# The last two layers of a fused attention, expert and feed-forward kernel, regrouped: four token tiles a group, the middle values in chunks of 256, the sums of a group held in four banks of PSUM

## The chip, the cores and the metric

The kernel runs on one core of one Trainium2 chip. The metric is the device time of one execution in microseconds (us); lower is better. PE is TensorE's matmul queue, PEld its weight loads, DVE is VectorE, ACT ScalarE, POOL GpSimd and SP SyncE. Matmul results go to PSUM, which has eight banks of 512 float32 values in each of 128 partitions.

## The reference, cut to what matters

Three layers follow each other: a linear attention, a mixture of experts that picks two of eight experts for each token, and a dense feed-forward layer. The change is in the last.

```python
x = attention(q, k, v)                    # 2304 tokens of 512 values
x = mixture_of_experts(x)                 # top 2 of 8 experts, 512 -> 1024 -> 512
# the dense layer: w_in is 512 x 2048, w_out is 2048 x 512
h = x @ w_in
g = np.maximum(h, 0.0) + alpha * np.minimum(h, 0.0)
return (g @ w_out).astype(np.float32)
```

## The kernel before

The tokens are cut into 18 tiles of 128 rows, called T0 to T17. Every matrix product is made of three matmuls, since each operand is kept as a high part and a low part (`xh` and `xl`, `gh` and `gl`, `hi` and `lo`): high by high, low by high, high by low. The parts are written by two engines in turn: ACT rounds a value to its high part, then DVE or POOL subtracts that from the value to get the low part.

The dense layer has two steps. `ffn_in` multiplies the inputs by `w_in` and gives the 2048 middle columns in sixteen slices of 128, here called f0 to f15. Each slice is a block of twelve matmuls into one PSUM bank, with the weights held in the array and the tokens streaming past. Two DVE instructions read the bank (lines 940 and 941: the negative part, then the sum with the positive part, into a tile `neg`). ACT makes `gh` from `neg` (line 942) and POOL makes `gl` (line 943). `ffn_out` multiplies the middle values of one tile by `w_out`: 48 matmuls with a moving width of 512 into one bank, then ACT copies the sums to `y` and sends them to memory.

In the kernel before, a group is two tiles, so a matmul of `ffn_in` streams 256 columns, and nine groups follow each other. A group does all of `ffn_in` (192 matmuls), then `ffn_out` for its two tiles. All banks of sums come from a rotation of five (`acc_tile`), so that PE can be up to five slices ahead of DVE.

Between them lies the preparation of the next group. `gather_y` fetches for each tile the two expert outputs of its tokens, which are called a and b here, by indirect DMAs from POOL (tile name `xg`, four buffers). `mix` scales a on ACT (line 856) and adds b on DVE (line 857). `turn` transposes the sum on PE into `pt` and writes `xh` and `xl`.

Two more things happen beside the first group alone. The weights `w_out` are still to be split into high and low parts: eight pieces of 128 x 1024, a cast on ACT (line 165) and a subtraction on DVE or POOL (line 166) each. And `maybe_overflow` has every engine read a counter and branch, for the case that an expert got more tokens than its buffer holds; with these inputs the branch is not taken. An engine that passes the branch adjusts the semaphores for the work it skipped, so that a later wait for that engine can end only when it has passed too. In the code before, the branch is written in the middle of the second `ffn_out` of the first group.

After the expert layers the order on each engine is set by a scheduler that works on priorities in program order; it may move an instruction past others on its engine.

Of the kernel before, what the change touches and what calls it, by code (L numbers as in the profile page):

```python
# [8 lines left out]
F32 = mybir.dt.float32  # L9
# [13 lines left out]
LT = LOW // 128  # L23
# [3 lines left out]
EPS = 1e-9  # L27
NVA = 2
NKV = 6
TG = 2  # L30
GROUP = TG * 128
LAST = NT - 2
TINY = 1.125 * 2.0 ** -15

# [13 lines left out]
def r(ap):  # L48
    return ap.bitcast(F32R)
# [3 lines left out]
def attention_moe_ffn(ctx, tc, q, k, v, w_gate, w_noise, noise, w1, w2, w_in, w_out, alpha, out):  # L53
# [16 lines left out]
    turns, held = [0], [None]  # L70

    def acc_tile():

        if turns[0] % 5 == held[0]:
            turns[0] += 1
# [656 lines left out]
    def drain(share):  # L732

        credit[0] += share * credit[1]
        while fill and fill[0][0] <= credit[0] + 0.3:
            w, fn = fill.pop(0)
            credit[0] -= w
            fn()

    def split(i, vector=4):  # L740

        return [(1.14, lambda j=j: split_piece(i, j, nc.vector if j < vector else nc.gpsimd)) for j in range(4)]
# [96 lines left out]

        return [(0.94, one), (1.28, two), (0.6, three)]  # L840

    def gather_y(g):
        for c in range(TG):
            T = g * TG + c
            src = ys[0:E * LOW, :] if (T + 1) * 128 <= LOW else ys[0:E * CAP, :]
            for i in range(2):
                t = xg[g, c, i] = moe.tile([128, DM], F32, name="xg", bufs=4)
# [4 lines left out]
    def mix(g, c):  # L852

        T = g * TG + c
        a, b = xg[g, c, 0], xg.pop((g, c, 1))
# [3 lines left out]
    def turn(g, c):  # L859
        sl = slice(g % 2 * GROUP + c * 128, g % 2 * GROUP + (c + 1) * 128)  # L860
        split_t(xg.pop((g, c, 0)), xh[:, :, sl], xl[:, :, sl])

    doubles = [(i, j) for i in range(4) for j in range(8)] if wide else []
    pieces = list(doubles)
# [28 lines left out]
    for e in range(E):  # L893
        last = e + 1 == E
        plan(split(2 * e + 2), convert_next(3 if e else 0))
        if not last:
            fetch(e + 1, range(0 if e else LT, 4))
        if 0 < e < E - 1:
            expert_in(e, (0, 1))
        elif last:  # L900
            expert_in(e, [0])
            for c in range(LT):
                expert_out(e, c)
            gather_y(0)
            expert_in(e, [1])
        else:
            expert_in(e, [1])
        drain(9)
        plan(split(2 * e + 3), convert_next(3 if e else 0))
        for c in range(CT):  # L910
            prefetch(e + 1, c)
            if last and c == LT:
                for i in range(TG):
                    mix(0, i)
            elif last and c > LT:
                turn(0, c - LT - 1)
# [7 lines left out]
    early_cx.close()  # L924
    ffn = ctx.enter_context(tc.tile_pool(name="ffn", bufs=1))

    GT = []

    def ffn_in(g):
        GT[:] = [ffn.tile([128, F2 // 128, GROUP], F32, name=n) for n in ("gh", "gl")]  # L930
        xs0 = slice(g % 2 * GROUP, (g % 2 + 1) * GROUP)
        for f in range(F2 // 128):
            hi, lo = wt[2 * E + f // 8]
            acc = acc_tile()
            a = acc[:, :GROUP]
            mm3(a, [((hi[:, d * 1024 + f % 8 * 128:d * 1024 + f % 8 * 128 + 128],
                      lo[:, d * 1024 + f % 8 * 128:d * 1024 + f % 8 * 128 + 128]),
                     (xh[:, d, xs0], xl[:, d, xs0])) for d in range(4)])
            t = ffn.tile([128, GROUP], F32, name="neg", bufs=5)
            nc.vector.tensor_scalar(t, a, 0.0, alph[:, f:f + 1], op0=OP.min, op1=OP.mult)  # L940
            nc.vector.scalar_tensor_tensor(t, a, 0.0, t, op0=OP.max, op1=OP.add)  # L941
            nc.scalar.copy(r(GT[0][:, f, :]), t)  # L942
            nc.gpsimd.tensor_sub(r(GT[1][:, f, :]), t, GT[0][:, f, :])  # L943
            drain(0.08)

    def out_rows(T):
        hb, i = divmod(T, 9)
# [7 lines left out]
    def ffn_out(g, c, between={}):  # L955
        acc = acc_tile()
        cs = slice(c * 128, (c + 1) * 128)
        pairs = []
        for f in range(F2 // 128):
            hi, lo = wt[2 * E + 2 + f // 8]  # L960
            ws = slice(f % 8 * 512, (f % 8 + 1) * 512)
            pairs.append(((GT[0][:, f, cs], GT[1][:, f, cs]), (hi[:, ws], lo[:, ws])))
        mm3(acc, pairs, between)
        y = moe.tile([128, DM], F32, name="y", bufs=2)
        nc.scalar.copy(y, acc)  # L965
        for p, dst in out_rows(g * TG + c):
            nc.scalar.dma_start(dst, y[p])

    def overflow():


        wa = ffn.tile([128, 4096], F32, name="wa", tag="gh")
        wb = ffn.tile([128, 4096], F32, name="wb", tag="gl")
# [68 lines left out]
        for e in range(E):  # L1042
            n = nc.values_load(more[0:1, e:e + 1], min_val=0, max_val=MORE)
            with tc.For_i(0, n, 1) as tt:
                idx = ffn.tile([128, 2], I32, name="oidx")
                nc.sync.dma_start(idx, ls[bass.ds(e * ALL + CAP + tt * 128, 128), :])
                nc.sync.dma_start(wa.rearrange("p (a n) -> p a n", a=4),
                                  w1[e].rearrange("(a p) n -> p a n", p=128))
                nc.sync.dma_start(wb.rearrange("p (a n) -> p a n", a=8),
                                  w2[e].rearrange("(a p) n -> p a n", p=128))  # L1050
                x = moe.tile([128, DM], F32, name="y", bufs=2)
                nc.gpsimd.indirect_dma_start(out=x, out_offset=None, in_=xs[:, :],
                                             in_offset=bass.IndirectOffsetOnAxis(ap=idx[:, 0:1], axis=0))
                pt = ps.tile([128, 4, 128], F32, name="pt", bufs=2)
                for d in range(4):
                    nc.tensor.transpose(pt[:, d, :], x[:, d * 128:(d + 1) * 128], ident)
                xt = stage.tile([128, 4, 128], F32, name="oxt", tag="raw")
                nc.vector.tensor_copy(xt, pt)
                h = stage.tile([128, 8, 128], F32, name="oht", tag="raw")
                for f in range(8):  # L1060
                    acc = acc_tile()
                    for d in range(4):
                        nc.tensor.matmul(acc[:, 0:128], wa[:, d * 1024 + f * 128:d * 1024 + f * 128 + 128],
                                         xt[:, d, :], start=(d == 0), stop=(d == 3))
                    nc.scalar.activation(h[:, f, :], acc[:, 0:128], AF.Relu)
                acc = acc_tile()
                for f in range(8):
                    nc.tensor.matmul(acc, h[:, f, :], wb[:, f * 512:(f + 1) * 512],
                                     start=(f == 0), stop=(f == 7))
                y = moe.tile([128, DM], F32, name="y", bufs=2)  # L1070
                nc.scalar.copy(y, acc)
                nc.gpsimd.indirect_dma_start(
                    out=ys[:, :], out_offset=bass.IndirectOffsetOnAxis(ap=idx[:, 1:2], axis=0),
                    in_=y, in_offset=None)

    def maybe_overflow():
        n = nc.values_load(more[0:1, E:E + 1], min_val=0, max_val=MORE)
        at = turns[0]
        held[0] = (at - 1) % 5
        with tc.If(n > 0):  # L1080
            overflow()
        turns[0], held[0] = at, None

    for g in range(NTOK // GROUP):
        if g + 1 < NTOK // GROUP:
            gather_y(g + 1)
        if g == 0:
            plan(split(2 * E + 2) + split(2 * E + 3, 1))
        ffn_in(g)
        drain(9)  # L1090
        for c in sorted(range(TG), key=lambda c: g * TG + c == LAST):
            if g + 1 < NTOK // GROUP:
                mix(g + 1, c)
                turn(g + 1, c)
            ffn_out(g, c, {8: maybe_overflow} if g == 0 and c == TG - 1 else {})


_INS = ["q", "k", "v", "moe_w_gate", "moe_w_noise", "moe_noise", "moe_w1", "moe_w2",
# [22 lines left out]
```

## Time and profile before

| what | us |
|---|---|
| median of three runs | 995.37 |
| lowest and highest run | 994.95, 998.21 |
| the profiled execution, its time | 998.39 |
| its span, first to last instruction | 996.6 |
| its mean granted TensorE clock | 0.981 |

The profile shows the profiled execution, which is 3.02 us above the median; 1.79 us of its time lie outside its span. The dense layer begins 584.27 us after the first instruction.

### The profile page before, as it was taken

The numbers are of one execution on the slowest core, as the hardware profiler recorded it, in microseconds if no ns is written. First come the engines' busy times: TensorE is split into PE (matmuls) and PEld (weight loads), VectorE is DVE, ScalarE is ACT, GpSimd is POOL, SyncE is SP. The second block draws the span as 40 slices with busy tenths as digits, with TensorE's granted clock in tenths as the row PEclk, the third lists the DMA queues.
The fourth block names the chain that finished last, engine by engine and source line by source line (L and its number), as shares of the span: only waits on it lengthen the run. The fifth ranks groups of instructions, "written<-read, shape, count | busy, mean of one in ns | idle before, by whom it ended". The sixth has DMA issues, their size and how long they took to land. (4 is left out here: it accounts for less than half of the span.)

```text
span 996.6 us, 14925 instructions
## 1 busy us (share of the span) xinstructions
PE 953.0 (96%) x5882; PEld 860.0 (86%) x5882; DVE 508.0 (51%) x1005; ACT 317.3 (32%) x603; POOL 307.0 (31%) x333
## 2 busy tenths in 40 slices
PE   4876799999999999999999999999999999999998
PEld 3765689998989898898988998989898989989896
DVE  6777563666757666666623354425161524334150
ACT  3554423433334333333333343212121222212120
POOL 6662730022212231312100127533251424323140
PEclk9986799999999999999999999999999999999999
DMA  9871643657656675756444262310101010100000
GB/s 251 247 215 54 213 146 124 191 164 239 192 184 205 181 240 162 244 171 200 149 136 136 81 200 70 88 51 14 53 15 61 15 50 22 43 22 11 11 12 21
DMA packets 65168, 121.77 MB, mean 122 GB/s; under 512 B 13488, under 2 KB 30400, under 8 KB 65088
## 3 DMA queue, kind: packets, MB, share of 16 engines
q1 hardware_dynamic: 49120, 83.98, 28.0%
q0 software_dynamic: 6080, 19.67, 6.4%
q10 hardware_dynamic: 9888, 17.08, 4.6%
q8 instruction: 48, 0.79, 0.3%
q14 instruction: 32, 0.26, 0.1%
HBM read 92.65 MB, written 28.05 MB: 121 GB/s over the span
## 5 line engine op out<-in xcount | busy, mean ns | idle before, releaser
L755 PE MATMUL mm<-xh,hi 128*128 128x256 f32 (+1 forms) x1088 | 318.4, 293 | 1.6 <-PEq L1080 0.9
L755 PE MATMUL mm<-xh,lo 128*128 128x256 f32 (+1 forms) x1088 | 318.3, 293 | 0.0
L755 PE MATMUL mm<-xl,hi 128*128 128x256 f32 (+1 forms) x1088 | 318.3, 293 | 0.0
L755 PEld LDWEIGHTS mm<-xh,hi 128*128 128x128 f32 x1088 | 205.8, 189 | 3.2 <-issue 1.3
L755 PEld LDWEIGHTS mm<-xl,hi 128*128 128x128 f32 x1088 | 205.3, 189 | 0.8
L755 PEld LDWEIGHTS mm<-xh,lo 128*128 128x128 f32 x1088 | 205.0, 189 | 0.0
L943 POOL TENSOR_TENSOR gl<-neg,gh 128x256 fp32r<-128x256 f32 x144 | 107.3, 750 | 166.1 <-ACT gh L942 164.8
L166 DVE TENSOR_TENSOR lo<-raw,hi 128x1024 fp32r<-128x1024 f32 x69 | 84.5, 1229 | 107.5 <-ACT hi L165 106.9
L940 DVE TENSOR_SCALAR neg<-mm,alph 128x256 f32<-128x256 f32 x144 | 69.2, 482 | 126.7 <-PE mm L755 124.7
L755 PE MATMUL mm<-hi,hh 128*128 128x512 f32 (+1 forms) x320 | 129.1, 403 | 0.0
L755 PE MATMUL mm<-hi,hl 128*128 128x512 f32 (+1 forms) x320 | 125.8, 393 | 0.0
L755 PE MATMUL mm<-lo,hh 128*128 128x512 f32 (+1 forms) x320 | 125.8, 393 | 0.0
L833 POOL TENSOR_TENSOR cva<-cva,raw 128x512 int32<-128x512 int32 x32 | 43.9, 1371 | 235.1 <-DVE raw L831 137.2
L755 PE MATMUL mm<-hi,gh 128*128 128x512 f32 x288 | 113.6, 394 | 0.0
L755 PE MATMUL mm<-hi,gl 128*128 128x512 f32 x288 | 112.3, 390 | 0.0
L755 PE MATMUL mm<-lo,gh 128*128 128x512 f32 x288 | 112.1, 389 | 0.0
L942 ACT CAST gh<-neg 128x256 fp32r<-128x256 f32 x144 | 57.6, 406 | 126.8 <-DVE neg L941 119.9
L780 ACT ACTIVATE hh<-mm 128x368 fp32r<-128x368 f32 (+1 forms) x128 | 54.9, 431 | 129.1 <-PE mm L755 119.7
L165 ACT CAST hi<-raw 128x1024 fp32r<-128x1024 f32 x80 | 83.2, 1047 | 28.0 <-DMA raw<-in_moe_w_dram 10.8
L781 DVE SCALAR_TENSOR_TENSOR hl<-mm,hh 128x368 fp32r<-128x368 f32 (+1 forms) x128 | 60.7, 479 | 57.8 <-ACT hh L780 57.4
L848 POOL DMA_INDIRECT xg<-ys,yidx x36 | 34.6, 962 | 157.8 <-DMA ys<-y 83.5
L709 DVE TENSOR_TENSOR xl<-pt,xh 128x512 fp32r<-128x512 f32 (+1 forms) x58 | 39.3, 678 | 69.2 <-ACT xh L706 68.9
(157 smaller groups left out, 1117.4 us busy)
## 6 DMA issues: line engine op xcount, KB each, us to landing
raw<-in_moe_w_dram SPq DMA_DIRECT2D x60, 512.0 KB, 3.9
ys<-y ACTq DMA_DIRECT2D x32, 256.0 KB, 2.0
raw<-in_moe_w_in_dram SPq DMA_DIRECT2D x16, 512.0 KB, 4.6
wc<-cvm SPq DMA_DIRECT2D x32, 256.0 KB, 4.9
raw<-in_moe_w_out_dram SPq DMA_DIRECT2D x16, 512.0 KB, 4.3
raw<-wc SPq DMA_DIRECT2D x16, 512.0 KB, 3.9
kr<-in_k_dram SPq DMA_DIRECT2D x8, 512.0 KB, 6.8
qr<-in_q_dram SPq DMA_DIRECT2D x8, 512.0 KB, 8.4
```

Source lines behind the costliest of these rows:

```text
L165: nc.scalar.copy(r(hi[:, sl]), raw)
L166: lo_eng.tensor_sub(r(lo[:, sl]), raw, hi[:, sl])
L709: nc.vector.tensor_sub(r(lo), pt, hi)
L755: nc.tensor.matmul(acc, r(a), r(b), start=(n, k) == steps[0], stop=(n, k) == steps[-1])
L780: nc.scalar.activation(r(hh[:, f, :]), acc[:, :n], AF.Relu)
L781: nc.vector.scalar_tensor_tensor(r(hl[:, f, :]), acc[:, :n], 0.0, hh[:, f, :], op0=OP.max, op1=OP.subtract)
L833: nc.gpsimd.tensor_tensor(a, a, low, op=OP.add)
L848: nc.gpsimd.indirect_dma_start(out=t, out_offset=None, in_=src, in_offset=bass.IndirectOffsetOnAxis(ap=yidx[:, i, T:T + 1], axis=0))
L940: nc.vector.tensor_scalar(t, a, 0.0, alph[:, f:f + 1], op0=OP.min, op1=OP.mult)
L942: nc.scalar.copy(r(GT[0][:, f, :]), t)
L943: nc.gpsimd.tensor_sub(r(GT[1][:, f, :]), t, GT[0][:, f, :])
```

## The change

There are now five groups, of 2, 4, 4, 4 and 4 tiles, so `ffn_in` streams 512 columns in four of them. The middle values are no longer all made before they are used: chunk k holds two slices (`FC = 2`), f0 and f1 in chunk 0 and so on to chunk 7. For each k, PE does `ffn_in` of chunk k and then `ffn_out` of the chunk before, for all tiles of the group; each tile's sums stay in a bank of their own from the first chunk to the last. That takes four banks, two hold transposes, and the two left are the only ones for `ffn_in`: even slices always go to `bank`, odd ones to the bank with tag `mm4`. `neg` has three buffers in place of five. The split of the eight pieces of `w_out` is issued by hand, two pieces ahead of each of the chunks 0 to 3. The gathers of the next group come in two halves at k = 0 and 4, `mix` at 2 and 6, `turn` at 3 and 7, and the branch of `maybe_overflow` at k = 4 of the first group. `xh2` and `xl2` are new, a second place for a group's inputs.

```diff
-TG = 2
-GROUP = TG * 128
+GROUPS = (2, 4, 4, 4, 4)
+FC = 2
...
-    def ffn_in(g):
-        GT[:] = [ffn.tile([128, F2 // 128, GROUP], F32, name=n) for n in ("gh", "gl")]
-        xs0 = slice(g % 2 * GROUP, (g % 2 + 1) * GROUP)
-        for f in range(F2 // 128):
+    other = [ffn.tile([128, 4, 512], F32, name=n) for n in ("xh2", "xl2")]
+    places = [[xh[:, :, 0:512], xl[:, :, 0:512]], other]
+    first = [sum(GROUPS[:g]) for g in range(len(GROUPS))]
+
+    def ffn_in(g, k):
+
+        n = GROUPS[g] * 128
+        gh, gl = (ffn.tile([128, FC, 512], F32, name=m, bufs=2) for m in ("gh", "gl"))
+        ph, pl = places[g % 2]
+        for i in range(FC):
+            f = k * FC + i
             hi, lo = wt[2 * E + f // 8]
-            acc = acc_tile()
-            a = acc[:, :GROUP]
+            a = (ps.tile([128, 512], F32, name="mm", tag="mm4") if i else bank)[:, :n]
             mm3(a, [((hi[:, d * 1024 + f % 8 * 128:d * 1024 + f % 8 * 128 + 128],
                       lo[:, d * 1024 + f % 8 * 128:d * 1024 + f % 8 * 128 + 128]),
-                     (xh[:, d, xs0], xl[:, d, xs0])) for d in range(4)])
-            t = ffn.tile([128, GROUP], F32, name="neg", bufs=5)
+                     (ph[:, d, :n], pl[:, d, :n])) for d in range(4)])
+            t = ffn.tile([128, 512], F32, name="neg", bufs=3)[:, :n]
...
+    def ffn_out(g, k, gh, gl):
+
+        tiles = sorted(range(GROUPS[g]), key=lambda c: first[g] + c == LAST)
+        for c in tiles:
+            if k == 0:
+                sums[c] = bank_of(c)
+            cs = slice(c * 128, (c + 1) * 128)
+            for i in range(FC):
+                f = k * FC + i
+                hi, lo = wt[2 * E + 2 + f // 8]
+                ws = slice(f % 8 * 512, (f % 8 + 1) * 512)
+                for j, (a, b) in enumerate(((gh, hi), (gh, lo), (gl, hi))):
+                    nc.tensor.matmul(sums[c], r(a[:, i, cs]), r(b[:, ws]), start=(f == 0 and j == 0),
+                                     stop=(f == F2 // 128 - 1 and j == 2))
+            if (k + 1) * FC == F2 // 128:
+                y = moe.tile([128, DM], F32, name="y", bufs=2)
+                nc.scalar.copy(y, sums.pop(c))
...
+    def next_group(g, k):
+
+        if g + 1 == len(GROUPS):
+            return
+        T0, p = first[g + 1], places[(g + 1) % 2]
+        half = lambda c: range(T0 + c, T0 + c + 2)
+        if k == 0:
+            gather_y(*half(0))
+        elif k == 4:
+            if g == 0:
+                maybe_overflow()
+            gather_y(*half(2))
+        elif k in (2, 6):
+            for T in half(k // 4 * 2):
+                mix(T)
+        elif k in (3, 7):
+            for T in half(k // 4 * 2):
+                turn(T, T - T0, *p)
+
+    weights = split(2 * E + 2) + split(2 * E + 3, 1)
+    done = None
+    for g in range(len(GROUPS)):
+        for k in range(F2 // 128 // FC):
+            next_group(g, k)
+            for _ in range(min(2, len(weights))):
+                weights.pop(0)[1]()
+            made = ffn_in(g, k)
+            if done:
+                ffn_out(*done)
+            done = (g, k, *made)
+    ffn_out(*done)
```

How this moves instructions on the engines is shown at three places. The first is DVE at the start of the dense layer, where the first group's slices are read from PSUM (`neg<-mm` or `neg<-bank`), the pieces of `w_out` are split (`lo<-raw,hi`) and T2 and T3 are mixed (`xg<-xg,gates`). Before:

```order
L166 TENSOR_TENSOR lo_5549<-raw,hi_5548 128x1024 x3
L940 TENSOR_SCALAR neg<-mm,alph 128x256 x2
L941 SCALAR_TENSOR_TENSOR neg<-mm,neg 128x256 x2
L940 TENSOR_SCALAR neg<-mm,alph 128x256 x2
L941 SCALAR_TENSOR_TENSOR neg<-mm,neg 128x256 x2
L940 TENSOR_SCALAR neg<-mm,alph 128x256 x2
L941 SCALAR_TENSOR_TENSOR neg<-mm,neg 128x256 x2
L166 TENSOR_TENSOR lo_5549<-raw,hi_5548 128x1024
```

And DVE at the same place now:

```order
L164 TENSOR_TENSOR lo_5513<-raw,hi_5512 128x1024 x3
L941 TENSOR_SCALAR neg<-bank,alph 128x256
L941 TENSOR_SCALAR neg<-mm,alph 128x256
L942 SCALAR_TENSOR_TENSOR neg<-bank,neg 128x256
L942 SCALAR_TENSOR_TENSOR neg<-mm,neg 128x256
L164 TENSOR_TENSOR lo_5513<-raw,hi_5512 128x1024
L853 SCALAR_TENSOR_TENSOR xg<-xg,gates 128x512 x2
L941 TENSOR_SCALAR neg<-bank,alph 128x256
L164 TENSOR_TENSOR lo_5619<-raw,hi_5618 128x1024
L942 SCALAR_TENSOR_TENSOR neg<-bank,neg 128x256
L941 TENSOR_SCALAR neg<-mm,alph 128x256
L942 SCALAR_TENSOR_TENSOR neg<-mm,neg 128x256
```

Three pieces still stand ahead of the first slice; behind the second slice there are now a piece, both mixes and another piece, where six slices were read one after the other before.

The second place is POOL around the branch of `maybe_overflow` in the first group: the last low parts ahead of it, the read of the counter, the compare (what only a taken branch would run is left out), and what follows once it is passed. Before:

```order
L943 TENSOR_TENSOR gl<-neg,gh 128x256 x3
L1077 TENSOR_LOAD more
L1080 COMPARE_AND_BRANCH
...
L1080 UNCONDITIONAL_BRANCH
L848 DMA xg<-ys,yidx 128x512 x4
L943 TENSOR_TENSOR gl<-neg,gh 128x256 x2
```

And POOL around the branch now:

```order
L944 TENSOR_TENSOR gl<-neg,gh 128x256 x3
L1093 TENSOR_LOAD more
L1094 COMPARE_AND_BRANCH
...
L1094 UNCONDITIONAL_BRANCH
L845 DMA xg<-ys,yidx 128x512 x4
L944 TENSOR_TENSOR gl<-neg,gh 128x256 x3
```

The rows read nearly alike, but before, all sixteen low parts of the first group stand ahead of the branch and the two behind it belong to the next group; now eight stand ahead of it (f0 to f7), and those behind the four gathers are f8, f9 and f10 of the same group.

The third place is PE ahead of the same branch. Before:

```order
L755 MATMUL mm<-hi_5670,gh 128x512
L755 MATMUL mm<-lo_5671,gh 128x512
L755 MATMUL mm<-hi_5670,gl 128x512
L1077 TENSOR_LOAD more
L1080 COMPARE_AND_BRANCH
```

And PE ahead of the branch now:

```order
L973 MATMUL mm<-hi_5512,gh 128x512
L973 MATMUL mm<-lo_5513,gh 128x512
L973 MATMUL mm<-hi_5512,gl 128x512
L753 MATMUL bank<-xh,hi_5372 128x256
L1093 TENSOR_LOAD more
L1094 COMPARE_AND_BRANCH
```

Before, PE had finished the whole first group there; now it has done the chunks 0 to 3 of `ffn_out` and chunk 4 of `ffn_in`, and one matmul of f10, and the rest of the group follows.

## Rows read from the trace of the kernel before

**Rows 1.** The page: busy time, share of the span and instructions of PE.
```profile
PE 953.0 (96%) x5882; PEld 860.0 (86%) x5882; DVE 508.0 (51%) x1005; ACT 317.3 (32%) x603; POOL 307.0 (31%) x333
```

**Rows 2.** The chain that ended last: start us, us, what.
```profile
665.32 33.57 PE mm L755 x240
698.89 0.44 PE pt L705 x4
699.33 10.90 PE mm L755 x48
```

**Rows 3.** Timeline of PE, 550 to 588: start us, us, engine, line, operation, tiles.
```profile
550.49 0.33 PE L755 MATMUL mm<-xh,hi 128*128 128x368 f32 x1
...
566.65 0.40 PE L755 MATMUL mm<-hi,hh 128*128 128x512 f32 x1
...
572.00 0.40 PE L755 MATMUL mm<-hi,hl 128*128 128x512 f32 x1
...
584.27 0.28 PE L755 MATMUL mm<-xh,hi 128*128 128x256 f32 x1
...
587.10 0.28 PE L755 MATMUL mm<-xh,hi 128*128 128x256 f32 x1
```

**Rows 4.** Timeline of DVE, 584 to 603; in brackets the idle time before, and its releaser.
```profile
586.03 3.50 DVE L166 TENSOR_TENSOR lo<-raw,hi 128x1024 fp32r<-128x1024 f32 x3 [3.69 <-ACT hi L165]
589.45 0.87 DVE L940 TENSOR_SCALAR neg<-mm,alph 128x256 f32<-128x256 f32 x2
590.24 0.75 DVE L941 SCALAR_TENSOR_TENSOR neg<-mm,neg 128x256 f32<-128x256 f32 x2
...
601.83 0.78 DVE L857 SCALAR_TENSOR_TENSOR xg<-xg,gates 128x512 f32<-128x512 f32 x1
```

**Rows 5.** Timeline of ACT, 584 to 600.
```profile
595.57 0.72 ACT L856 ACTIVATE xg<-xg,gates 128x512 f32<-128x512 f32 x1 [2.40 <-DMA xg<-ys,yidx]
```

**Rows 6.** Timeline of POOL, 584 to 600.
```profile
592.01 0.95 POOL L848 DMA_INDIRECT xg<-ys,yidx  x1 [0.30 <-issue]
592.98 1.44 POOL L943 TENSOR_TENSOR gl<-neg,gh 128x256 fp32r<-128x256 f32 x2
```

**Rows 7.** The tile `xg`, 584 to 640: its ten gathers, from issue to landing.
```profile
DMA to landing us min/median/max: 3.4/3.7/5.4
```

**Rows 8.** Line 1077, the read of the counter, by engine queue: duration ns, start us.
```profile
L1077 DVEq TENSOR_LOAD <-more x1: 800/800/800, 619.5 to 619.5; - x1
L1077 PEldq TENSOR_LOAD <-more x1: 490/490/490, 625.5 to 625.5; - x1
```

**Rows 9.** Line 1080, the branch and the semaphores adjusted behind it.
```profile
L1080 DVEq EVENT_SEMAPHORE  x2: 21/21/21, 623.3 to 623.4; - x2
```

**Rows 10.** Timeline of all engines, 623.5 to 631.
```profile
623.59 0.96 POOL L848 DMA_INDIRECT xg<-ys,yidx  x1 [7.96 <-DVEq L1080]
...
627.36 0.95 POOL L848 DMA_INDIRECT xg<-ys,yidx  x1 [0.30 <-issue]
...
629.37 0.39 PE L755 MATMUL mm<-hi,gl 128*128 128x512 f32 x1
...
630.67 0.36 PE L755 MATMUL mm<-xh,hi 128*128 128x256 f32 x1 [0.92 <-PEq L1080]
```

**Rows 11.** Timeline of ACT and its DMA queue, 980 to 997.
```profile
982.54 1.14 ACTq L967 DMA_DIRECT2D out_dram<-y  x2
...
993.42 0.34 ACTq L967 DMA_DIRECT2D out_dram<-y  x1
```

**Rows 12.** Windows: us, each engine's busy time (instructions), then PEclk, DMA share, GB/s.
```profile
0.00:20.00 20.00, 8.02 (x34) 6.02 (x35) 11.00 (x13) 5.30 (x7) 13.14 (x42) 1.00 0.97 250
48.00:60.00 12.00, 7.86 (x36) 7.06 (x35) 6.69 (x15) 7.05 (x15) 10.36 (x8) 0.72 1.06 292
```

**Rows 13.** Timeline of PE in these windows.
```profile
8.47 0.47 PE L256 MATMUL pk<-ident,m 128*128 128x128 f32 x1 [2.65 <-DVE m L244]
...
52.72 0.33 PE L357 MATMUL bank<-ident,kv 128*128 128x128 f32 x1 [3.75 <-ACT kv L350]
```

More of the change, by code (lines that the diff above doesn't have):

```diff
@@ L69, in attention_moe_ffn @@
     bank = gps.tile([128, 512], F32, name="bank")
-    turns, held = [0], [None]
+    turns = [0]
     def acc_tile():
-        if turns[0] % 5 == held[0]:
-            turns[0] += 1
         i = turns[0] % 5
@@ L840, in convert, with gather_y @@
         return [(0.94, one), (1.28, two), (0.6, three)]
-    def gather_y(g):
-        for c in range(TG):
-            T = g * TG + c
+    def gather_y(*tiles):
+        for T in tiles:
             src = ys[0:E * LOW, :] if (T + 1) * 128 <= LOW else ys[0:E * CAP, :]
             for i in range(2):
-                t = xg[g, c, i] = moe.tile([128, DM], F32, name="xg", bufs=4)
+                t = xg["y", T, i] = moe.tile([128, DM], F32, name="xg", bufs=4)
                 nc.gpsimd.indirect_dma_start(
@@ L903, in attention_moe_ffn @@
                 expert_out(e, c)
-            gather_y(0)
+            gather_y(*range(GROUPS[0]))
             expert_in(e, [1])
@@ L912, in attention_moe_ffn @@
             if last and c == LT:
-                for i in range(TG):
-                    mix(0, i)
+                for T in range(GROUPS[0]):
+                    mix(T)
             elif last and c > LT:
-                turn(0, c - LT - 1)
+                turn(c - LT - 1, c - LT - 1, xh, xl)
             if c >= LT or 0 < e < E - 1:
@@ L953, in out_rows, with bank_of, quarters @@
                 for u in range(2)]
[L955 to L967, printed above, removed]
+    sums = {}
+    def bank_of(i):
+        return (gps if i < 3 else ps).tile([128, 512], F32, name="mm", tag=f"mm{i}")
+    def ffn_out(g, k, gh, gl):
[14 more added lines that the diff above has]
+                nc.scalar.copy(y, sums.pop(c))
+                for p, dst in out_rows(first[g] + c):
+                    nc.scalar.dma_start(dst, y[p])
     def overflow():
-        wa = ffn.tile([128, 4096], F32, name="wa", tag="gh")
-        wb = ffn.tile([128, 4096], F32, name="wb", tag="gl")
+        def quarters(name):
+            return [ffn.tile([128, 1024], F32, name=f"{name}{j}", tag=("gh", "gl")[j // 2], bufs=2) for j in range(4)]
         flat, used = stage.tile([128, 1024], F32, name="calc", tag="raw"), [0]
@@ L1046, in overflow @@
                 nc.sync.dma_start(idx, ls[bass.ds(e * ALL + CAP + tt * 128, 128), :])
[L1047 to L1050, printed above, removed]
+                wa = quarters("wa")
+                for j in range(4):
+                    nc.sync.dma_start(wa[j], w1[e, j * 128:(j + 1) * 128, :])
                 x = moe.tile([128, DM], F32, name="y", bufs=2)
@@ L1077, in maybe_overflow @@
         n = nc.values_load(more[0:1, E:E + 1], min_val=0, max_val=MORE)
-        at = turns[0]
-        held[0] = (at - 1) % 5
         with tc.If(n > 0):
             overflow()
[L1082 to L1095, printed above, removed]
+    def next_group(g, k):
[11 more added lines that the diff above has]
+            for T in half(k // 4 * 2):
+                mix(T)
+        elif k in (3, 7):
[13 more added lines that the diff above has]
+    ffn_out(*done)
 _INS = ["q", "k", "v", "moe_w_gate", "moe_w_noise", "moe_noise", "moe_w1", "moe_w2",
```

30 lines of the change are left out of this document (16 added, 14 removed).

## The prediction

> **What bounds the kernel now.** I read the page first: PE is busy for 953.0 of 996.6 us [rows 1]. The chain of waits says where the end is made: from 630 us on it is one line of PE work, with nothing of another engine in it until the last copy [rows 2]. So the dense layer costs what PE's instructions cost, and three pitches give it. A block of 48 matmuls of width 512 takes 10.90. A block of 240 takes 33.57, so the 192 of width 256 in it take 22.67, or 0.1181 each, and those of width 512 take 0.2271. A transposed tile takes 0.44 [rows 2]. Nine groups make 9 x 22.67 = 204.0, eighteen tiles 18 x 10.90 = 196.2, sixteen turned tiles 16 x 0.44 = 7.0. At the branch of the first group 1.30 lie between two starts, 1.07 more than the pitch [rows 10]. The sum is 408.3, from 584.27 [rows 3] to 992.6. PE loses nothing else in this layer, so a change can gain only by fewer or cheaper matmuls, and loses whatever it makes PE wait.
>
> **What the wider matmuls save.** Eight of nine 192-blocks of width 256 become four of width 512: 768 matmuls fewer, the same columns. The trace has no matmul of `ffn_in` of width 512. The nearest rows differ. `ffn_out` has 0.2271. In the last expert, 96 matmuls of width 368 lie between 550.49 and 566.65, 0.1683 each, and 23 steps of width 512 between 566.65 and 572.00, 0.2326 each [rows 3]. A straight line from 256 over 368 to 512 meets the second. Eight old blocks are 181.4; four new ones are 768 x 0.2271 = 174.4 or 768 x 0.2326 = 178.6, so the saving is 7.0 or 2.8. One row has the layer in its favour, the other the line through the form with `xh`, so I take the middle, **4.9**. `ffn_out` keeps its 864 matmuls, in another order; I leave them at 0.2271, since slices before change banks without a gap. At 0.2326 they would cost 4.7 more, the outer end.
>
> The Trainium skill (TensorE: Matmul & The Clock Gate, Back-to-back issue gap) puts the gap of warm matmuls at the columns over 2.4 GHz plus 2.5 ns, so a merged pair would save only 2.5 ns, in all 1.9 us as an estimate. The rows here show 11 to 19 ns above the columns' time, not 2.5, so the measured pitches stand.
>
> **What it costs: PE waits in the first group.** The new order gives `ffn_in` two banks in place of five, so slice f2 can't begin before f0 has been read. I follow PE, DVE, ACT and POOL through the group in the order shown in the change, with durations from the rows.
>
> First wait. DVE's three split pieces run from 586.03 to 589.5, since ACT can cast the first only behind the last expert's copy; the order keeps them ahead of f0. Then come two reads and the first of two sums: 589.45 to about 590.66 [rows 4]. f2 follows f1 in the array, so PE could start it at 587.10 [rows 3]. It starts at 590.75: **3.65**. Before, three more banks covered this; that cover is gone.
>
> Second wait. DVE next has a piece and the mixes of T2 and T3, and only then f2. ACT's scaling of T3 began at 595.57, when its gather landed, and took 0.72 [rows 5]; the other gather was issued at 592.01 [rows 6] and lands 3.4 to 5.4 later [rows 7], 595.4 to 597.4. I take 596.5. Behind it on DVE stand the mix (0.78), the first read of f2 (0.44), a piece (3.50 / 3 = 1.17) and the sum of f2 (0.38) [rows 4]: f4 can begin at about 599.4. PE comes from 590.75 through f2 and f3 (24 x 0.118 = 2.8) and the first chunk of `ffn_out` (12 x 0.227 = 2.7) to 596.3. **3.1**, with ends 2.9 and 4.0.
>
> Third wait. Two lots of work now cross the branch in mid-group: the low parts of f8 and f9 stand on POOL behind the branch and behind four gathers. Before, POOL was held at its gather until 623.59 by DVE's passing of the branch [rows 10]. DVE had begun reading the counter at 619.5 [rows 8], and adjusted its semaphores at 623.4 [rows 9]. So 4.1 pass from DVE's last instruction to POOL's first gather, 4.7 from there to the end of the fourth (627.36 + 0.95) [rows 10], and 0.7 for a low part (1.44 / 2) [rows 6]. DVE comes to the counter about 0.8 after PE ends f9, as its last sum begins. So f8's low part is there 0.8 + 4.1 + 4.7 + 0.7 = 10.3 after f9. PE meanwhile does a chunk of `ffn_out` (2.7), the branch (1.1 to 1.8), f10 and f11 (2.8), and two matmuls that need only the high part (0.45): 7.5. **2.8**, with ends 2.0 and 3.5. Before, nobody asked for low parts behind the branch until the next group.
>
> The branch itself: PE's queue read the counter at 625.5 [rows 8], 3.9 ahead of its last matmul at 629.37 [rows 10]; now fewer long matmuls stand ahead of it, so less of it is covered: **0.4** more (0 to 0.8). Smaller waits follow, as gathers hang on mixes, mixes on gathers, and ACT's casts stand behind them: I take **0.7** in all, and 0 to 4. From the second group on a chunk gives the others 24 x 0.23 + 24 x 0.227 = 11 us for two slices; DVE needs some 1.4 for each even at twice the present width, so banks, `gh` and `gl` are in time. The waits sum to **10.65**, with ends 8.55 and 15.95.
>
> The end: four tiles finish 1.36 apart where two finished 10.9 apart, `y` has two buffers, and T17's two transfers hold ACT's queue for 1.14 against 0.34 [rows 11]. The last copy begins later by at most 0.8; I take **0.6**.
>
> **The clock.** In the first 20 us PE waited 2.65 once and the granted clock stayed at 1.00; in 48 to 60, where it waited 3.75, the mean was 0.72 [rows 12, 13]: part of it at the lower of the two levels, 1.2 GHz, which costs 12 x 0.28 = 3.4 of full-speed time. The new waits lie between. What falls after the first is hidden by the second, which is set by a gather; behind the second and third I take 1.0 each, **2.0** (0 to 6.7). The Trainium skill (TensorE: Matmul & The Clock Gate, HAM oscillation — how this bites in real kernels) says that waits between bursts of matmuls send the array back to half clock, so that the penalty is paid after each. By that each wait would be dearer; that is the third rival.
>
> **The sum.** -4.9 + 10.65 + 0.6 + 2.0 = +8.35 on the profiled span of 996.6, so 1004.95, and 1006.7 as that execution's time. It stood 3.02 above the median; from the median of 995.37 the forecast is **1003.7**.
>
> **The rivals.** What can be told from no change is some 0.3%, or 3 us: 992.4 to 998.4.
> - *Faster.* The place is f2's and f4's banks and POOL behind the branch: if DVE and POOL are ahead of PE there, all three waits go, and the time is 995.37 - 4.9 + 0.4 + 0.7 + 0.6 = 992.2, or 990.1 at the lower pitch. It decides once the three together stay under 1.9. Against it stand three pieces fixed ahead of f0 and the gathers ahead of f8. 0.08.
> - *No change.* Only the first wait is real: gathers land early and POOL isn't held. +3.65 + 1.7 - 4.9 gives 995.8. For it speaks that the second hangs on one landing and the third on how the branch holds POOL; against it, both are seen in rows. 0.16.
> - *The clock falls for long* after two waits, each as in 48 to 60: 3.4 x 2 in place of 2.0, 1008.4. 0.10.
> - *Waits return in every half group*, since a mix that waits for a gather holds ACT's casts and DVE's reads: seven more half groups at 1.2, the 0.38 of a sum and the 0.78 of a mix, are 8.4, so 1012. The slack of some 4 us in each chunk speaks against it. 0.07.
>
> **How the numbers follow.** My forecast has 0.59, with its own range of 999 to 1009. With every term at its low end (-7.0 + 8.55 + 0 + 0) it is 996.9, with every one at its high end (-2.8 + 15.95 + 0.8 + 6.7) 1016. The range of 994 to 1012 takes in the second and third rivals, and leaves out the faster one (0.08), the dearer half of the last (0.04) and the far corner of the high ends. Faster: 0.08. Same: the second rival and the low edge of the forecast, 0.17. Slower: 0.75.
>
> **What would show it.** In the profile after, PE should idle before `bank<-xh,hi` for about 3.6 near 587 and 3 near 596, released by DVE, and before a matmul with `gl` for about 3 near 621, released by POOL; later groups should show PE without gaps, a width-512 pitch of `ffn_in` between 0.227 and 0.233, and PE's matmuls 768 fewer. I am wrong if the three waits sum to under 5, if the new pitch is under 0.225, or if PE loses more than 3 in groups two to five.

## The result and the profile after

The changed kernel takes 1007.97 us (median of 4 runs, 1006.10 to 1010.50), the kernel before 995.9 beside it. The ratio is 1.0119 with an interval of 1.0089 to 1.0150: slower by 12 us. The forecast was 1003.7, with a range of 994 to 1012, and slower at 0.75.

The profiled execution after took 1007.01 us with a span of 1005.2, the one before 998.39 and 996.6. Those two are only 8.6 apart: the stretch ahead of the layer, whose work is the same, took 584.27 before and 582.22 after. So lengths inside the layer are used below, from the first matmul of `ffn_in` to the last of `ffn_out` plus one pitch. Before it is 584.27 to 992.6, 408.3 [rows 3]; after it is 582.22 to 1000.74, 418.5. The dense layer is 10.2 longer.

The page, after:

```profile
PE 953.0 (95%) x5114; PEld 825.0 (82%) x5114; DVE 483.6 (48%) x877; ACT 305.2 (30%) x539; POOL 294.1 (29%) x269
```

768 matmuls are gone [rows 1], and PE is exactly as long busy. The view of waits of PE, 580 to 1006 (tile and line, releaser: total us, times, longest):

```profile
PE bank L753 <- DVE neg L942: 6.1, 2, 3.4
PE mm L973 <- POOL gl L944: 2.1, 1, 2.1
PE bank L753 <- PEq L1094: 1.1, 1, 1.1
```

In the layer PE waits four times, and no more after 626. The timeline of PE shows where:

```profile
584.93 0.28 PE L753 MATMUL mm<-xh,lo 128*128 128x256 f32 x1
588.65 0.39 PE L753 MATMUL bank<-xh,hi 128*128 128x256 f32 x1 [3.44 <-DVE neg L942]
...
593.11 0.40 PE L973 MATMUL mm<-hi,gh 128*128 128x512 f32 x1
...
598.67 0.38 PE L753 MATMUL bank<-xh,hi 128*128 128x256 f32 x1 [2.64 <-DVE neg L942]
...
619.37 0.36 PE L753 MATMUL bank<-xl,hi 128*128 128x256 f32 x1 [1.08 <-PEq L1094]
...
625.33 0.51 PE L973 MATMUL mm<-hi,gl 128*128 128x512 f32 x1 [2.06 <-POOL gl L944]
```

The first costs 3.60, from start to start less the pitch. Each of the others is a block of twelve matmuls that ends late, from its start to the start of the next block (593.11 to 598.67, 618.01 to 620.74, 622.17 to 627.29), less the twelve at their pitch: 2.83, 1.31 and 2.39. Behind the first two the clock falls. In the windows (the column after the engines' busy times is the granted clock):

```profile
582.00:590.00 8.00, 4.56 (x35) 4.31 (x34) 6.01 (x8) 4.69 (x6) 2.94 (x4) 0.97 0.41 130
590.00:600.00 10.00, 7.36 (x38) 6.50 (x38) 4.25 (x8) 4.52 (x8) 5.02 (x4) 0.84 0.50 171
600.00:615.00 15.00, 15.00 (x95) 13.94 (x94) 5.82 (x12) 4.60 (x8) 9.51 (x9) 0.89 0.20 66
615.00:640.00 25.00, 21.86 (x135) 18.95 (x134) 9.85 (x20) 6.39 (x13) 14.24 (x17) 1.00 0.34 97
```

f2 and f3 last from 588.65 to 593.11, 4.46 where 2.83 is the full-speed time of two slices of width 256; f4 and f5 last 4.40. That is 1.63 and 1.57, together 3.2. The mean of 0.84 is part of the stretch at the lower of the two levels, 1.2 GHz: matmuls of width 256 start 0.213 apart there (590.01, then 590.22), and 0.118 apart at full speed.

DVE's timeline shows why the first two waits are there. Three split pieces stand ahead of f0's read, and both mixes, each waiting for a gather, ahead of f2's:

```profile
583.99 3.50 DVE L164 TENSOR_TENSOR lo<-raw,hi 128x1024 fp32r<-128x1024 f32 x3 [3.69 <-ACT hi L163]
587.40 0.47 DVE L941 TENSOR_SCALAR neg<-bank,alph 128x256 f32<-128x256 f32 x1
...
592.57 0.75 DVE L853 SCALAR_TENSOR_TENSOR xg<-xg,gates 128x512 f32<-128x512 f32 x1 [2.50 <-DMA xg<-ys,yidx]
596.00 0.75 DVE L853 SCALAR_TENSOR_TENSOR xg<-xg,gates 128x512 f32<-128x512 f32 x1 [2.68 <-DMA xg<-ys,yidx]
596.67 0.48 DVE L941 TENSOR_SCALAR neg<-bank,alph 128x256 f32<-128x256 f32 x1
```

On POOL four gathers follow the branch, and the low parts only then:

```profile
619.82 0.96 POOL L845 DMA_INDIRECT xg<-ys,yidx  x1 [7.74 <-DVEq L1094]
...
624.54 2.62 POOL L944 TENSOR_TENSOR gl<-neg,gh 128x256 fp32r<-128x256 f32 x3
```

The chain of waits gives the new pitches (start, length, what; the first two rows are slices of width 512 through `xh2`, the third a chunk of `ffn_out` for four tiles):

```profile
639.56 2.80 PE bank L753 x12
...
673.64 2.80 PE mm L753 x12
676.44 5.45 PE mm L973 x24
```

A wide matmul of `ffn_in` takes 2.80 / 12 = 0.233, one of `ffn_out` 0.2271 as before [rows 2]. A block of 192 wide ones is 16 x 2.795 = 44.7, against 45.3 for the two narrow blocks that it replaces.

All of it together: 22.7 + 4 x 44.7 + 196.2 + 7.0 + 3.60 + 2.83 + 1.31 + 2.39 + 3.2 = 418.0 of the 418.5; another 0.4 is `ffn_out` between narrow slices, shown by the run with narrow groups below.

### The profile page after: what moved, and what is told of

Same layout as the page of the kernel before. It is cut to its first block, busy times and chain, and to the rows that moved or that the text cites. A ratio compares the mean times of both kernels' runs of the same rounds, so it can differ in the third digit from the quotient of the medians.

```text
span 1005.2 us, 13115 instructions
## 1 busy us (share of the span) xinstructions
PE 953.0 (95%) x5114; PEld 825.0 (82%) x5114; DVE 483.6 (48%) x877; ACT 305.2 (30%) x539; POOL 294.1 (29%) x269
## 5 line engine op out<-in xcount | busy, mean ns | idle before, releaser
L753 PE MATMUL mm<-xh,hi 128*128 128x256 f32 (+2 forms) x672 | 217.8, 325 | 1.0 <-ACT xh L704 0.7
L753 PE MATMUL mm<-xh,lo 128*128 128x256 f32 (+2 forms) x672 | 217.1, 324 | 0.0
L753 PE MATMUL mm<-xl,hi 128*128 128x256 f32 (+2 forms) x672 | 217.0, 324 | 0.0
L944 POOL TENSOR_TENSOR gl<-neg,gh 128x512 fp32r<-128x512 f32 (+1 forms) x80 | 94.4, 1183 | 225.7 <-ACT gh L943 225.2
L753 PEld LDWEIGHTS mm<-xh,hi 128*128 128x128 f32 x672 | 128.0, 191 | 7.8 <-ACT xh L704 1.1
L753 PEld LDWEIGHTS mm<-xl,hi 128*128 128x128 f32 x672 | 128.2, 191 | 6.2
L753 PEld LDWEIGHTS mm<-xh,lo 128*128 128x128 f32 x672 | 127.8, 191 | 5.7
L943 ACT CAST gh<-neg 128x512 fp32r<-128x512 f32 (+1 forms) x80 | 45.9, 576 | 241.8 <-DVE neg L942 229.7
L941 DVE TENSOR_SCALAR neg<-bank,alph 128x512 f32<-128x512 f32 (+1 forms) x40 | 27.8, 696 | 170.6 <-PE bank L753 170.6
L753 PEld LDWEIGHTS mm<-hi,hl 128*128 128x128 f32 (+1 forms) x320 | 59.3, 185 | 14.7
```

Source lines behind the costliest of these rows:

```text
L753: nc.tensor.matmul(acc, r(a), r(b), start=(n, k) == steps[0], stop=(n, k) == steps[-1])
L943: nc.scalar.copy(r(gh[:, i, :n]), t)
L944: nc.gpsimd.tensor_sub(r(gl[:, i, :n]), t, gh[:, i, :n])
```

## The experiments

The theory is that waits in the first group, and the clock behind them, make the loss. It had two rivals. One is that the waits are only where the loss becomes visible, and that regrouping itself costs the time (chunks, banks that change every six matmuls, groups of four). The other is that the helpers are too slow in the first group whatever the banks. In each run below, "the layer" is measured as above; 418.5 is the changed kernel.

**Four banks in the first group.** Its `ffn_in` uses the banks that two tiles of sums leave free.

```diff
-            a = (ps.tile([128, 512], F32, name="mm", tag="mm4") if i else bank)[:, :n]
+            if g == 0 and k % 2:
+                a = bank_of(2 + i)[:, :n]
+            else:
+                a = (bank_of(4) if i else bank)[:, :n]
```

> Edit of the changed kernel: in the first group alone, where only two banks hold sums, every second chunk of `ffn_in` uses the two banks that are still free, so that PE can be four slices ahead of DVE instead of two. Theory (the loss is the first two waits for a bank and the clock that falls behind them): f2 and f3 run at once behind f1; the wait moves to the first chunk of `ffn_out`, whose low parts stand on POOL behind four gathers and are there at 591.66 and 592.4 by the rows of the changed kernel, so the chunk ends near 594.0 in place of 595.84, and f4 follows at once, to end near 596.9 in place of 603.07: 6.2 us less in the layer, in all 1002, and the second wait (2.8) and most of the low clock (3.2) are gone. Rival (DVE, ACT and POOL are simply too slow in the first group, whatever the banks): PE waits for `gh` or `gl` instead, under 2 us less. Rival (regrouping itself costs, not the first group): no difference.

Measured: 1000.77, ratio to the kernel before 1.0053 (1.0035 to 1.0071); the layer 412.3, 6.2 less, as expected. The windows:

```profile
582.00:590.00 8.00, 6.30 (x48) 5.48 (x46) 6.47 (x9) 4.71 (x7) 4.35 (x5) 1.00 0.52 161
590.00:600.00 10.00, 9.71 (x62) 8.63 (x62) 6.70 (x12) 4.91 (x9) 7.10 (x7) 1.00 0.45 158
```

The clock stays at 1.00. What is left before 600 is 0.62 for a bank, 1.08 for `gh` and 0.29 for `gl`. Up to the transposes of T2 and T3 PE has gained 6.8; 0.6 of it are given back at the branch, which costs more here: 2.4, the largest wait left. So the agreement with 6.2 is in part luck. Two banks, with the order that goes with them, and the clock behind their waits are shown as the cause of 6 of the 10 us. Banks and order are not parted by this run: with four banks the scheduler also put DVE's reads of f2 and f3 ahead of the mixes.

**The first four chunks in an order by hand.** Two banks stay; the gathers stand behind the low parts of f0 and f1, the mixes one chunk later, the transposes of T2 and T3 behind chunk 3, and two split pieces instead of three ahead of f0.

```diff
-        elif k in (2, 6):
+        elif k in ((3, 6) if g == 0 else (2, 6)):
...
-            next_group(g, k)
+            if g == 0 and k == 0:
+                byhand.append(tc.manual_schedule())
+                byhand[0].__enter__()
+            if g or k:
+                next_group(g, k)
+            made = ffn_in(g, k)
+            if not g and not k:
+                next_group(g, k)
...
```

> Edit of the changed kernel: the order of the first group's first four chunks is written out by hand: two split pieces ahead of the reads of f0 instead of three, the low parts of f0 and f1 ahead of the gathers of T2 and T3 on POOL, the mixes of T2 and T3 behind the reads of f5 instead of ahead of f2; the two banks of `ffn_in` stay. Theory (the waits are made by what stands ahead of the reads on DVE): the first wait falls from 3.6 to about 2.0, the second from 2.8 to 0, and the clock costs 0 to 1.6 instead of 3.2: 6.0 to 7.7 us less, 1000 to 1002. Rival (two banks are too few in any order): PE still waits in front of f4, under 2 us less. Rival (the clock falls for a reason other than the waits): the 3.2 stay, 4.5 less.

Measured: 1006.41, ratio 1.0104 (1.0087 to 1.0121); the layer 418.5, nothing gained. The first wait fell from 3.60 to 2.40 from start to start (2.2 in the view), and the second, in front of f4, went, as the theory has it; the clock stays at 1.00 up to 615. But PE's waits are these now, 580 to 1006:

```profile
PE pt L703 <- DVE xg L853: 2.8, 1, 2.8
PE mm L973 <- POOL gl L944: 2.6, 2, 2.1
PE bank L753 <- DVE neg L942: 2.4, 2, 2.2
PE bank L753 <- PEq L1094: 2.1, 1, 2.1
```

The transposes of T2 and T3 wait for the later mixes, the branch costs more, and the clock falls behind the wait for `gl` (0.81 in 624 to 632). The expectation counted the waits it removed, and not what was late next. So it is shown that the order on DVE sets the first two waits, and also that setting it alone gains nothing.

**The gathers of T4 and T5 a chunk later.**

```diff
-        elif k == 4:
-            if g == 0:
-                maybe_overflow()
+        elif k == 4 and g == 0:
+            maybe_overflow()
+        elif k == (4 if g else 5):
             gather_y(*half(2))
```

> Edit of the changed kernel: the gathers of T4 and T5 are written one chunk later (k 5 instead of 4), so that on POOL one gather and not four stands between the branch and the low parts of f8 and f9. Theory (the third wait is POOL's gathers behind the branch): the low part of f8 is there near 621.8 instead of 625.3, before PE asks for it at 623.3; the wait of 2.4 goes and none comes in its place, since the mixes of T4 and T5 are due four chunks' halves later: 2.4 less in the trace's layer. Rival (the passing of the branch itself, 4.1 from DVE to POOL, is late enough): PE still waits, 1 us or less is gained. Rival (a later mix holds ACT and DVE in the next group): as much is given back before 660.

Measured: 1008.14, ratio 1.0120 (1.0103 to 1.0137); the layer 418.6. The low parts of f8 and f9 come at 620.74, and PE doesn't wait there any more: gathers ahead of low parts are shown as the cause of the third wait. But the second rival, that as much is given back before 660, held too. At 634 the mix that waits for a late gather stands on DVE between the two reads of a slice, and PE waits 1.8 for that bank:

```profile
633.72 0.75 DVE L853 SCALAR_TENSOR_TENSOR xg<-xg,gates 128x512 f32<-128x512 f32 x1 [3.15 <-DMA xg<-ys,yidx]
634.39 0.42 DVE L942 SCALAR_TENSOR_TENSOR neg<-mm,neg 128x256 f32<-128x256 f32 x1
```

**Narrow groups for the last twelve tiles.**

```diff
-GROUPS = (2, 4, 4, 4, 4)
+GROUPS = (2, 4, 2, 2, 2, 2, 2, 2)
...
-        if g + 1 == len(GROUPS):
+        if g + 1 == len(GROUPS) or k > 3 and GROUPS[g + 1] == 2:
```

> Edit of the changed kernel: the first two groups stay as they are (two and four tiles), the other twelve tiles are six groups of two, in the same chunks and the same banks. So three of the four blocks of `ffn_in` of width 512 become six of width 256, 576 matmuls more. Theory (the width saves only what the measured pitches give, 192 x 0.2329 = 44.7 for a wide block and 2 x 22.67 = 45.3 for two narrow ones): 0.6 a block, 1.9 us more, all of it in groups three to eight. Rival (the wide blocks save as much as forecast, 1.2 a block, and something else of the regrouping eats it): 3.7 more, or less if the narrow groups also lose that something. Rival (groups of four cost PE time in waits): it gets faster.

Measured: 1009.85, ratio 1.0151 (1.0120 to 1.0183); the layer 421.7, 3.2 more, with no wait behind the first group. From start to start in the timeline of PE, from the first wide slice on, `ffn_in` takes 180.6 against 179.4 and `ffn_out` 179.2 against 177.4. So the width of three blocks gives 1.2, or 0.4 a block, less than either theory had, and `ffn_out` the rest, which neither had: its rows read 2.78 for 12 matmuls between narrow slices, 5.45 for 24 between wide ones. Groups of four do not cost PE time by themselves.

**Two banks in the kernel before.**

```diff
-            acc = acc_tile()
+            acc = acc_tile() if g else ps.tile([128, 512], F32, name="mm", tag=f"mm{3 + f % 2}")
```

> Edit of the kernel before: in its first group alone `ffn_in` rotates over two banks instead of five; all else stays, the mixes too, which stand behind the group's sixteen slices there. Theory (two banks alone, with three split pieces ahead of the first read, make the first wait): PE stops in front of f2 for 3 to 4 us, the clock may fall once behind it (up to 1.6), and no second wait of this size follows, since no mix stands between the reads: 3.5 to 5.5 slower than the kernel before, near 1000.5. Rival (in this order DVE reads in time or the slack is taken up later): under 1 slower.

Measured: 1010.46, ratio 1.0152 (1.0121 to 1.0183); the layer 420.4, 12 more than before, over twice the expectation. PE's timeline:

```profile
588.27 0.38 PE L755 MATMUL mm<-xh,hi 128*128 128x256 f32 x1 [3.44 <-DVE neg L941]
593.14 0.63 PE L705 MATMUL pt<-ident,xg 128*128 128x128 f32 x4 [0.25 <-DVE xg L857]
596.44 0.66 PE L705 MATMUL pt<-ident,xg 128*128 128x128 f32 x2 [2.67 <-DVE xg L857]
598.21 0.58 PE L755 MATMUL mm<-xh,hi 128*128 128x256 f32 x1 [1.11 <-DVE neg L941]
```

and in the windows the clock is down to 0.67:

```profile
590.00:600.00 10.00, 5.97 (x29) 5.19 (x28) 4.18 (x7) 4.62 (x9) 5.09 (x4) 0.67 0.48 163
```

The first wait is the one of the changed kernel to the hundredth, 3.44. What the expectation missed is that with two banks the scheduler put both mixes ahead of DVE's reads of f2 here too, and transposes between PE's slices, and that these then wait for gathers. So this run shows that taking banks away is enough for a loss of this size, without chunks or wider groups, though not through one mechanism alone.

**Which operand sets the pitch.** In the third group the held weights come from `gh` and `gl`, in the fourth the streamed columns from `w_out`.

```diff
...
+            if g == 2:
+                left = [(done[2][:, d % 2, 0:128], done[3][:, d % 2, 0:128]) for d in range(4)]
+            if g == 3:
+                wh, wl = wt[2 * E + 2]
+                right = [(wh[:, d * 512:d * 512 + 512], wl[:, d * 512:d * 512 + 512]) for d in range(4)]
...
```

> Measures the pitch of a matmul of width 512, 0.2329 in `ffn_in` and 0.2271 in `ffn_out`. Edit of the changed kernel, whose output is another: in the third group the weights held in the array are taken from `gh` and `gl` instead of `w_in`, in the fourth the streamed columns are taken from `w_out` instead of `xh` and `xl`. If the pitch follows the streamed operand, the fourth group falls to 0.227 and the third stays; if it follows the held one, the third falls and the fourth stays; if it follows neither (the bank, the place in the program), both stay at 0.233. The time is within 1.5 us of the changed kernel in any case (192 x 0.0058 = 1.1).

Measured, one execution: 1010.45; the layer is 421.9, 3.4 more, all of it in the first group, which the edit leaves alone: its two waits for DVE sum to 8.1 instead of 6.1, the longest 4.6 instead of 3.4, where a split piece on DVE took 3.13 instead of 1.22, and the clock falls behind the wait for `gl` too (0.93 in 615 to 640). One execution doesn't show why. The fourth group keeps 44.9 for its 192 matmuls of `ffn_in`, as the second has. The third falls to 44.4, and its `ffn_out` rises from 0.2271 to 0.2289 a matmul. So, in this one execution, the streamed operand is not it. The held one moves a part, but `ffn_in` and `ffn_out` together stay the same (88.4 against 88.5). Where the 6 ns come from stays open.

**Towards a version that beats both.** The first group in chunks of four slices with four banks, in an order by hand up to the branch:

```diff
+        step = FC if g else 4
+        gh, gl = (ffn.tile([128, step, 1024 // step], F32, name=m, bufs=2) for m in ("gh", "gl"))
...
+            a = (bank_of((0, 4, 2, 3)[i]) if i else bank)[:, :n]
...
```

> A version meant to beat both: as the changed kernel from the second group on. In the first group chunks of four slices and four banks, the order written out by hand: low parts of f0 to f3 ahead of the gathers of T2 and T3, the mixes of T2 and T3 behind all reads of f0 to f7, their transposes behind the first two chunks of `ffn_out`, the branch behind that, and then eight slices before the next chunk of `ffn_out` asks for a low part. Theory (the whole difference to the kernel before is waits of the first group and the clock behind them, less the small saving of the width): with no wait but the branch (1.2 to 2.4) the layer is 22.7 + 178.9 + 196.2 + 7.0 + 1.2 to 2.4 = 406.0 to 407.2, which is 11 to 12.5 under the changed kernel and 1 to 2 under the kernel before: 994 to 996, the granted clock at 1.00 throughout. Rival (the regrouping has a cost of its own in later groups or at the end): it stays above the kernel before by 2 or more.

Measured: 1005.76, ratio 1.0100 (1.0079 to 1.0121); the layer 415.6. Up to 605 PE doesn't wait at all. Then come 2.7 at the branch, 2.5 and 0.8 for banks (DVE passes the branch late and then stands in a mix behind a gather), 1.6 for `xh`, and a clock of 0.93 between 615 and 640. The expected 994 to 996 failed at the branch, which had been priced as PE's own 1.2 to 2.4, without DVE's delay. The time is in the rival's range, but not for its reason: the last of these waits ends before 635, and PE doesn't wait after it. So the branch went behind 24 wide matmuls that PE does while the other engines pass it, and three split pieces that POOL had done went to DVE:

> As the version with long chunks, and its order carried on by hand to the end of the first group: the transposes of T2 and T3 stand inside the second chunk of `ffn_out`, the branch directly behind that chunk, so that PE has 24 matmuls of width 512 in front of it while the other engines reach it; all remaining split pieces stand ahead of the branch, on DVE; the gathers of T5 stand behind the low parts of f8 to f11, and T4 and T5 are turned behind the last chunk of `ffn_out`. Theory (what was left of the loss in the version with long chunks, 2.7 at the branch, 2.5 and 0.8 for a bank behind it, 1.6 for xh and some 1.5 of clock, comes from where the branch and the late mixes stand): these go but for about 1.2 at the branch and up to 1 for f12's bank; the layer is 22.7 + 178.9 + 196.2 + 7.0 + 1.2 to 2.2 = 406.0 to 407.0, against 408.3 before, so 994 to 995.5, level with or 1 to 2 us under the kernel before. Rival (passing the branch costs its 4 us on whichever engine PE needs next, wherever it stands): waits of 5 us or more stay behind it, 998 or more.

Measured: 1002.63, ratio 1.0062 (1.0048 to 1.0076); the layer 414.2. The wait at the branch fell to 1.5, near the theory's 1.2, but the theory's total of 994 to 995.5 did not come true. The rival's, 998 or more, did, by luck: what is left is not the passing of the branch but one wait of 4.1 at the start of the second group. There the scheduler had put a scaling for the next group, which waits for a gather, ahead of ACT's casts to `xh`, and behind that wait the clock falls:

```profile
631.18 0.72 ACT L852 ACTIVATE xg<-xg,gates 128x512 f32<-128x512 f32 x1 [4.30 <-DMA xg<-ys,yidx]
...
632.79 1.07 ACT L704 CAST xh<-pt 128x512 fp32r<-128x512 f32 x2 [0.42 <-ACT y L981]
```

```profile
632.00:640.00 8.00, 6.08 (x16) 4.90 (x17) 2.64 (x4) 2.66 (x5) 1.90 (x2) 0.58 0.46 135
```

So the order was held by hand to the end. Its core:

```diff
...
+    piece()
+    order = tc.manual_schedule()
+    order.__enter__()
+    gather_y(2)
+    a = ffn_in(0, 0)
+    gather_y(3)
+    piece()
+    b = ffn_in(0, 1)
+    piece()
+    ffn_out(0, 0, *a)
+    both(mix, 2)
+    ffn_out(0, 1, *b, lambda: (both(turn1, 2), piece()))
+    maybe_overflow()
+    gather_y(4)
+    a = ffn_in(0, 2)
+    gather_y(5)
+    b = ffn_in(0, 3)
+    both(mix, 4)
+    ffn_out(0, 2, *a)
+    both(turn1, 4)
+    ffn_out(0, 3, *b)
...
```

> As the version with the branch covered, but the order is held by hand to the end of the program, and T4 and T5 are turned between the third and the fourth chunk of `ffn_out`. In that version PE lost 1.5 at the branch, then 4.1 where the casts to xh of T4 and T5 stood on ACT behind a scaling that waited for the gather of T7, and some 3 of clock behind that (0.58 between 632 and 640). Theory (those are all that is left between it and the kernel before): 6.5 to 7.5 us go, the layer is 22.7 + 178.9 + 196.2 + 7.0 + 1.5 = 406.3, the clock 1.00 throughout, the time 994 to 996. Rival (the late groups need the scheduler's order, mixes ahead of reads as soon as gathers land): new waits in the second to fifth group, 998 or more. Rival (two buffers of `y`, 0.5 at the end, and the wide pitch leave nothing to win): 996 to 998, level with before.

Measured: 995.78 against 997.99 beside it, ratio 0.9979 (0.9966 to 0.9991): faster than the kernel before, by about 2 us (0.9 to 3.4 by the interval). All of PE's waits in the layer:

```profile
PE bank L753 <- PEq L1098: 1.3, 1, 1.3
PE pt L703 <- DVE xg L853: 0.3, 1, 0.3
```

The windows show the clock at 1.00 throughout:

```profile
582.00:590.00 8.00, 8.00 (x71) 8.00 (x70) 5.81 (x10) 3.92 (x7) 4.60 (x6) 1.00 0.32 97
590.00:600.00 10.00, 10.00 (x56) 8.68 (x55) 7.75 (x12) 5.89 (x10) 6.11 (x7) 1.00 0.49 162
600.00:615.00 15.00, 13.40 (x97) 11.90 (x96) 9.82 (x17) 5.21 (x10) 4.76 (x6) 1.00 0.34 108
615.00:640.00 25.00, 25.00 (x126) 21.00 (x126) 9.75 (x16) 6.43 (x13) 11.43 (x13) 1.00 0.28 85
```

The layer is 407.2, from 581.04 to 988.2, against 408.3 before. This is the test of the whole account: with the first group's waits gone, all of the loss is gone, and no cost of regrouping itself is left to find. The 1.1 in the layer fit the small saving of the width, less the 0.7 by which the two waits exceed the 0.9 that PE waits in the kernel before. The other 1 us of the 2 is not in the layer. The kernel before measured 995.9 to 996.6 beside the other runs and 997.99 here, so that other 1 us may be no gain at all. No run holds the old groups in an order by hand, so that the gain needs groups of four is argued and not shown.

## Why the prediction was right, point by point

*Direction and mechanism* were right: all three waits are there, in the order, at the tiles and with the releasers that were named, and no wait comes later. Four banks and the order by hand take away or shorten the first two, later gathers the third.

*The saving* is the term that was mis-sized. It was taken as 4.9, the middle of 2.8 and 7.0. By 0.2329 it is 181.4 - 178.8 = 2.6, the end that followed the line through the form with `xh`; and the first group's `ffn_out` gives 8 x 2.78 - 21.8 = 0.4 of that back between its narrow slices. The row that shared the operand was the better guide than the row of the same layer. The run with narrow groups has even less, 0.4 a block or 1.6 for four.

*The waits*: 3.65, 3.1 and 2.8 were forecast, 3.60, 2.83 and 2.39 measured; the branch adds 0.2 where 0.4 was taken. Of the 0.7 of smaller waits nothing is seen. Together the waits are 1.6 less than forecast.

*The clock* was taken as 2.0, none of it behind the first wait and 1.0 behind each of the others. It fell for 1.63 behind the first and 1.57 behind the second, and not behind the third. The reasoning on the first fits: f4 can't start before DVE has read f2, so a faster f3 would have met a longer wait. But that wait did not end where it was placed: f4 began 16.45 after the layer's start, not 15.1. The last gather for T3, issued at 589.97, landed 5.9 later, where the rows had 3.4 to 5.4, and the mix waited for it. So at full speed the second wait would have been 4.46, above its upper end of 4.0; the low clock filled 1.63 of it. The Trainium skill (TensorE: Matmul & The Clock Gate, HAM oscillation — how this bites in real kernels) describes a kernel whose array falls back to half clock in each long wait for a transfer between its bursts of matmuls, so that the penalty is paid every time; here the clock fell behind the waits of 3.44 and 2.64 and not behind the one of 2.06.

One row behind the clock's term was misread. The 1.00 of the first 20 us [rows 12] is no sign that the clock stayed up behind a wait of 2.65: PE also waited 5.16 and 2.41 there, and eight matmuls of 130 columns took 1.73 from 15.88 to 17.61, eight of the same shape 0.89 from 25.76 to 26.65. So the array ran at about half its later speed there, though the column prints 1.00, and that row is no support for a small term of the clock.

*The end*: 0.6 taken. From PE's last matmul to the end of the span are 1005.2 - 1000.74 = 4.46, against 996.6 - 992.6 = 4.0: 0.46. The last four copies go by two buffers of `y`:

```profile
998.22 0.59 ACT L977 COPY y<-mm 128x512 f32<-128x512 f32 x1 [0.77 <-PE mm L973]
...
999.69 0.59 ACT L977 COPY y<-mm 128x512 f32<-128x512 f32 x1 [0.88 <-DMA out_dram<-y]
...
1001.54 0.58 ACT L977 COPY y<-mm 128x512 f32<-128x512 f32 x1 [1.27 <-DMA out_dram<-y]
```

The forecast sum was 8.35; the layer and the end give 10.2 + 0.46 = 10.7, 2.3 more. The saving that was not there makes 2.7 of it (4.9 against 2.6 less 0.4). The waits were 1.6 too high and the clock 1.2 too low, and that these two nearly cancel is luck. The forecast median lies 4.3 under the measured one: besides the 2.3, the kernel before measured 0.5 more beside the change than in the three runs that the forecast began from, and the remaining 1.4 is the scatter between single profiled executions and medians.

## What to carry to other kernels

Before banks are given to something else, see what stands on the engine that empties them, in its own order, between two of its reads: the depth in banks has to cover that, and here three split pieces and two mixes behind gathers were 3.4 and 2.6 us too long for two banks. A wait that is removed alone can come back one step later, as the order by hand and the later gathers show. Four banks alone took back 6 of 10 us; the rest, and a time below the kernel before, came only when banks, order, branch and gathers were set together, and each edit was followed to what is late next. Price a new shape of matmul by the row that shares its operands, as far as one case can teach it, and take the small end until it is measured.

## What was not expected of the hardware

- The clock. It fell behind waits of 3.44, 2.64 and 4.07 us (to 0.58 in 8 us), and stayed at 1.00 with 0.62, 1.08 and 0.29 before 600 and 2.44 at the branch in the run with four banks. A wait of 2.06 was followed by 1.00 in the changed kernel, and one of 2.07 by 0.81 in the run by hand; in that same run one of 2.76, for the mixes, was followed by 1.00. So the length of one wait does not decide it, and what does is not shown.
- A matmul of width 512 takes 0.2329 in `ffn_in` and 0.2271 in `ffn_out`, same widths, same types; by one execution the streamed operand is not the reason.
- The branch that is not taken makes PE wait 2.7 and 2.4 behind narrow slices, and 1.3 and 1.5 behind 24 wide matmuls. Behind 12 wide ones and a narrow one it was 1.1 in the changed kernel and 2.1 in the run by hand, so the matmuls ahead of it are not all that sets it.
